# Two transformer layers on one core: other key blocks, more exponentials on VectorE, one GELU moved

## The chip, the cores and the metric

The kernel runs on one core of one Trainium2 chip. The metric is the device time of the core in microseconds (us), the median over several executions. Where two kernels are compared, both ran on the same chip in the same rounds. The chips used for the experiments were not all the same one, and the kernel before ran between 1080.2 and 1083.6 us (medians) on them, so between chips only ratios of the same rounds are compared. On one chip its executions went from 1080.5 us at a granted clock of 0.998 to 1086.9 at 0.992; single profiles therefore differ by a few us for no reason in the kernel.

## The reference, cut to what matters

Two identical layers on 2048 rows of 448 numbers. Each is an attention block (16 heads of 28) and a mixer block with two GELUs.

```python
def _A_ref(x, wqkv, wo):            # attention
    ...
    scores = jnp.einsum("bhqd,bhkd->bhqk", q, k) * (Dh ** -0.5)
    p = _softmax(scores, axis=-1)
    o = jnp.einsum("bhqk,bhkd->bhqd", p, v)
    return ... @ wo

def _B_ref(x, w1, w2, w3, w4):      # mixer
    h = _gelu(_layernorm(x) @ w1)
    # four quarters of h are shifted by -1, +1, -2, +2 rows: hs
    x1 = x + hs @ w2
    return x1 + _gelu(_layernorm(x1) @ w3) @ w4

x = x + _A_ref(_layernorm(x), wqkv, wo); x = x + _B_ref(_layernorm(x), w1, w2, w3, w4)   # twice
```

The softmax has 2 x 16 x 2048 x 2048 exponentials; they are the largest single piece of work. The second layer's attention needs keys from all rows of the first layer's output, so at the crossing the first layer's mixer has to deliver in time.

## The kernel before

Rows are cut into 16 tiles of 128, queries into units of four tiles, heads into four groups of four. TensorE makes scores (keys on the partitions, 512 queries wide) in groups of two or three 512-column banks; ScalarE turns each group into exponentials with one instruction; TensorE multiplies these with the values. A "segment" is one unit, one head group and one block of keys. The first units of a layer work on blocks of keys as these become known; what a block gives is stored and merged later with a correction factor:

```python
ORDER = {0: [(0, 0), (0, 1), (0, 2)], 1: [(0, 0), (1, 0), (0, 1), (0, 2), (1, 1), (1, 2)]}   # (unit, block)
PARTS = {0: [(0, 4), (4, 8), (8, NT)], 1: [(0, 8), (8, 12), (12, NT)]}                      # key tiles of a block
```

Some groups leave their third score to VectorE, which makes the exponential with integer and polynomial steps in seven instructions:

```python
def on_dve(n):
    if len(grans[n]) < 3:
        return False
    L, u, g, p, kts, first, last = segs[grans[n][2][0]]
    return 1 <= grans[n][2][1] <= len(kts) * UNITS[L][u][1] // 4 - 4 and (104 < n < 300 and n % 8 == 0)

def t_dexp(n):
    # ...
    yield op("dve", 0.06 + c_ps(512), lambda e: e.tensor_scalar(out=t32[:, :], in0=ps[:, bk, :], scalar1=0.0, scalar2=65536.0, op0=ALU.max, op1=ALU.mult), ...)
    # five instructions on 512 columns of fp16, then the seventh writes the bf16 result
```

The mixer's second GELU is run in batches of tiles, each between two loads of ScalarE's function table. In `MIXB` an entry is (tiles, ..., batch):

```python
MIXB = [
    [([0, 1, 2], 0, 0), ([3, 4, 5, 6], 3, 0), ([7, 8, 9, 10], 0, 1), ([11, 12], 4, 2), ([13, 14, 15], 0, 2)],
    [([0, 1, 2], 4, 0), ([3, 4, 5, 6], 0, 0), ([7, 8, 9, 10], 3, 1), ([11, 12], 0, 1), ([13], 2, None), ([14, 15], 3, None)],
]
```

The mixer's weights come by four loads on SyncE's queue during the first layer's attention. The queries' normalized rows `xn` are turned into `xT` by a transposing DMA on the same queue:

```python
for (dst, src_, nm, w) in ((w1, B_w1, "w1", 112), (w3, B_w3, "w3", 112), (w2, B_w2, "w2", 112), (w4, B_w4, "w4", 128)):
    yield op("sp", 0.1, lambda e, ...: e.dma_start(...), writes=[(nm,)], dma=True, dma_time=12.0)

def transposes(xs, xt, n, on_pe=False):
    # ...
    yield op("sp", 0.1, lambda e: e.dma_start_transpose(...), reads=[xs.key, ("xnpad",)], writes=[xt.key], dma=True, dma_time=2.4 + 0.65 * n)
```

The program is not written in the order in which it runs. Every task yields operations with an assumed duration; an order-maker places them on the engines by priority, and `MOVES` is a list of (time, random number) by which it shakes the priorities. Such lists are found by search: the one with the shortest estimate is kept. The order of each engine is then fixed: in the stall shown below, TensorE waits 9.23 us for one product, and the scores that stand behind it come only after it. Where the order-maker expects TensorE idle, it puts in dummy products with an all-ones tile. They are meant to keep its granted clock up.

```python
for k in range(ROUNDS):
    res = attempt(plan)
    plan = res[2].latest_starts(res[0])
for moves in MOVES[:-1]:
    res = attempt(plan, moves)
    plan = res[2].latest_starts(res[0])
est, P, SC = attempt(plan, MOVES[-1])
```

A DMA has a fixed duration there: 2.4 + 0.65 x 4 = 5.0 us for a transposing DMA of four tiles.

Of the kernel before, what the change touches and what calls it, by code (L numbers as in the profile page):

```python
# [8 lines left out]
ALU = mybir.AluOpType  # L9
# [487 lines left out]
def build_kernel(nc, A_x, A_wqkv, A_wo, B_x, B_w1, B_w2, B_w3, B_w4, out, n_layers=2):  # L497
# [13 lines left out]
    DEFER = 4  # L511
    EXPC = (0.30457565 * 128, 0.07826797 * 128)
# [6 lines left out]
            (0.00, 991188), (12.02, 9652), (24.07, 779245), (36.31, 574974), (48.34, 995852), (133.26, 234581), (170.16, 377973), (182.64, 78779),  # L519
            (194.78, 320468), (218.87, 670156), (268.25, 22056), (280.26, 710161), (292.73, 679129), (304.89, 711509), (328.97, 386094), (382.28, 899246),  # L520
            (406.49, 746217), (418.70, 101258), (430.88, 346142), (443.17, 682745), (455.33, 932794), (467.35, 356989), (479.51, 744780), (510.52, 543020),
            (522.57, 402041), (534.73, 618216), (546.82, 418518), (558.83, 824624), (570.92, 353463), (624.44, 145788), (636.47, 941956), (648.52, 565007),
            (684.71, 872168), (697.00, 394582), (709.22, 683072), (745.71, 487532), (757.79, 818477), (770.17, 569389), (806.55, 126763), (818.66, 378060),
            (870.93, 441302), (907.43, 514310), (919.45, 887013), (931.49, 271738), (968.02, 708052), (980.04, 674587), (992.15, 577414), (1004.20, 157345),
            (1016.21, 778514), (1028.52, 870529), (1040.65, 657776), (1052.77, 892667),
# [8 lines left out]
    ORDER = {0: [(0, 0), (0, 1), (0, 2)], 1: [(0, 0), (1, 0), (0, 1), (0, 2), (1, 1), (1, 2)]}  # L534
# [7 lines left out]
        [([0, 1, 2], 4, 0), ([3, 4, 5, 6], 0, 0), ([7, 8, 9, 10], 3, 1), ([11, 12], 0, 1), ([13], 2, None), ([14, 15], 3, None)],  # L542
# [8 lines left out]
    PARTS = {0: [(0, 4), (4, 8), (8, NT)], 1: [(0, 8), (8, 12), (12, NT)]}  # L551
# [19 lines left out]
    with st:  # L571
# [40 lines left out]
        kmaxc = sb("kmaxc", [128, 2, 4, NCH], FP32)  # L612
# [3 lines left out]
        dcol = sb("dcol", [128, 2, NPART, 4], FP32)  # L616
        dbc = sb("dbc", [128, 2, NPART, 4], FP32)
        fct = sb("fct", [128, 2, NPART, 4], FP32)
# [248 lines left out]

        def kslot(L, c):
            return c if L % 2 == 0 else (4, 5, 0, 1)[c]
# [7 lines left out]
        def norm_x(tiles, xs):  # L877
            for i, t in enumerate(tiles):
                yield op("dve", 0.12 + c_b2b(D), lambda e, t=t, i=i: e.tensor_scalar(out=blk(xs.v[:, i, :]), in0=b112(x_res[:, t, :]), scalar1=mv[:, t, 0:1], scalar2=rstd[:, t:t + 1],
                                                                          op0=ALU.subtract, op1=ALU.mult),  # L880
                         reads=[("x", t), ("mv", t), ("rstd", t)], writes=[(xs.key, i)])
# [51 lines left out]
        def k_proj(L, c, g, xt):  # L933
            c0 = kcol(L, 4 * c)
            b2 = yield from kq_proj(xt, g, wk_pad, "wk_pad", kT[:, g, c0:c0 + 512], [("kT", g, vslot(L, 4 * c + i)) for i in range(4)], MK, ("cols",), 512, 1.0)
            yield op("dve", c_ps(512), lambda e, b2=b2: e.reduce_max(out=kmaxc[:, L, g, c:c + 1], in_=ps[:, bi(b2), :], axis=AX.X),  # L936
# [4 lines left out]
        def q_proj(L, u, g, xt):  # L941
# [4 lines left out]
            if u >= PU[L]:  # L946
                yield ("wait", ("bc", L, NPART - 1, g))
                bias, bkey = bcol[:, L, NPART - 1, g:g + 1], ("bcol", L, NPART - 1, g)
# [30 lines left out]
        def t_ln1(L, c):  # L979
            tiles = list(range(4 * c, 4 * c + 4))  # L980
# [28 lines left out]
            sl = slice(4 * c, 4 * c + 4)  # L1009
            yield op("dve", 0.1, lambda e: e.tensor_scalar(out=vpe[:, sl], in0=mv[:, sl, 1], scalar1=EPS, scalar2=None, op0=ALU.add),  # L1010
                     reads=[("mv", t) for t in tiles], writes=[("vpe", t) for t in tiles])
            yield op("pool", 1.0, lambda e: e.tensor_tensor(out=rstd[:, sl], in0=vpe[:, sl], in1=neghalf[:, 0:4], op=ALU.pow),
# [728 lines left out]
```

## Time and profile before

| | kernel before |
|---|---|
| time, median of 3 | 1080.63 us (1080.58 to 1082.69) |
| span of the profiled execution, granted clock | 1077.6 us, 1.0 |
| ScalarE busy | 1028.3 us, 95% |
| first to last softmax exponential | 27.1 to 1041.6 us |
| from the last one to the end (below: the tail) | 36.1 us |

The span is read as three parts: up to the first exponential, the phase from the first to the last exponential, in which ScalarE is nearly always busy, and the tail. The lines for this stand in the prediction below. One thing the prediction did not look at, and that matters later, is SyncE's queue around 150 us, when the queries of unit 1 of the first layer are prepared. The lines of that queue's timeline in the kernel before have start, duration of the issue on the queue, what is issued, and how many:

```profile
134.81 1.73 SPq L798 DMA_DIRECT2D wo_pad<-in_A_wo_dram  x4
136.59 2.26 SPq L801 DMA_DIRECT2D w<-in_B_w_dram  x4
149.91 16.58 SPq L852 DMA_TRANSPOSE xT<-xn  x2
```

The four weight loads are issued from 136.59 us; the transposing DMA follows 13 us later (the line covers it and the next one, which starts at 165 us). The view of the tile `xT` for 120 to 240 us says how long its three transposing DMAs took from issue to landing:

```profile
DMA to landing us min/median/max: 3.2/3.6/8.2
```

Two took some 3.5 us, the one behind the loads 8.2. By the same view TensorE waited 2.2 us for it, and ScalarE's longest wait for a score (L1212), 1.9 us at 157 us, follows from that.

### The profile page before, as it was taken

The numbers are of one execution on the slowest core, as the hardware profiler recorded it, in microseconds if no ns is written. First come the engines' busy times: TensorE is split into PE (matmuls) and PEld (weight loads), VectorE is DVE, ScalarE is ACT, GpSimd is POOL, SyncE is SP. The second block draws the span as 40 slices with busy tenths as digits, with TensorE's granted clock in tenths as the row PEclk, the third lists the DMA queues.
The fourth block names the chain that finished last, engine by engine and source line by source line (L and its number), as shares of the span: only waits on it lengthen the run. The fifth ranks groups of instructions, "written<-read, shape, count | busy, mean of one in ns | idle before, by whom it ended". The sixth has DMA issues, their size and how long they took to land.

```text
span 1077.6 us, 22234 instructions
## 1 busy us (share of the span) xinstructions
PE 1041.8 (97%) x9674; PEld 407.6 (38%) x9674; DVE 649.5 (60%) x1539; ACT 1028.3 (95%) x939; POOL 54.3 (5%) x76
## 2 busy tenths in 40 slices
PE   8999999999999899999999999999999999999998
PEld 5233333333333333334334333333333333444545
DVE  7976148753885456933797338346958332755734
ACT  5999999999999999999999999999999999999973
POOL 2000000000000000000001000000000000010000
PEclk9999999999999999999999999999999999999999
DMA  4222080000000010000111112213110001100000
GB/s 114 60 89 69 10 194 20 16 1 21 20 2 20 2 40 21 1 21 20 21 40 31 26 40 60 69 35 113 46 28 4 21 14 29 21 21 2 2 15 26
DMA packets 74330, 37.85 MB, mean 35 GB/s; under 512 B 59064, under 2 KB 67640, under 8 KB 74232
## 3 DMA queue, kind: packets, MB, share of 16 engines
q1 hardware_dynamic: 74232, 36.43, 13.0%
q8 instruction: 75, 1.23, 0.5%
q14 instruction: 23, 0.19, 0.1%
HBM read 13.75 MB, written 8.13 MB: 20 GB/s over the span
## 4 chain that ended last, share of the span: by engine, by line
ACT 58%; PE 36%; DVE 4%; DMA 1%; issue 0%; SPq 0%; POOL 0%; DVEq 0%
ACT PT L1238 51%; PE ps L649 11%; PE ps L1212 10%; PE ps L1287 8%; ACT h2T L1615 4%; PE ps L652 4%; PE ps L1651 3%; ACT gt L1401 1%; ACT L1238 1%; ACT L1615 1%; DMA h2T<-in_A_wqkv_dram 1%; DVE st L811 0%; DVE qT L952 0%; DVE kmaxc L936 0%; DVE sq L924 0%
## 5 line engine op out<-in xcount | busy, mean ns | idle before, releaser
L1238 ACT ACTIVATE PT<-ps 128x1024 bf16<-128x1024 f32 (+1 forms) x823 | 930.1, 1243 | 14.1 <-PE ps L1212 10.3
L1212 PE MATMUL ps<-qT,kT 32*128 32x512 bf16 (+1 forms) x2304 | 320.1, 360 | 13.7 <-ACT PT L1238 9.3
L1287 PE MATMUL ps<-PT,vaug 128*32 128x512 bf16 (+1 forms) x2286 | 256.5, 362 | 3.4 <-ACT PT L1238 2.4
L1212 PEld LDWEIGHTS ps<-qT,kT 32*128 32x128 bf16 x2304 | 80.1, 91 | 261.2 <-ACT PT L1238 158.7
L1651 PE MATMUL ps<-ones_bf 128*128 128x256 bf16 x1136 | 171.3, 278 | 1.3 <-DVE hot L683 1.1
L1577 DVE CAST h2T<-ps 128x512 bf16<-128x512 f32 (+2 forms) x126 | 73.6, 584 | 97.8 <-PE ps L649 55.1
L1651 PEld LDWEIGHTS ps<-ones_bf 128*128 128x128 bf16 x1136 | 94.9, 99 | 77.8 <-issue 58.3
L1287 PEld LDWEIGHTS ps<-PT,vaug 128*32 128x32 bf16 x2286 | 66.0, 94 | 131.6 <-issue 75.5
L649 PE MATMUL ps<-xT,w 112*128 112x512 bf16 (+6 forms) x535 | 108.7, 323 | 0.9 <-DVE h2T L1577 0.2
L652 PE MATMUL ps<-xT,w 112*32 112x512 bf16 (+3 forms) x964 | 73.6, 339 | 0.0
L649 PEld LDWEIGHTS ps<-xT,w 112*128 112x128 bf16 (+1 forms) x535 | 43.1, 105 | 45.0 <-issue 20.9
L649 PE MATMUL ps<-w,h2T 128*128 128x448 bf16 x250 | 58.8, 354 | 1.3 <-ACT h2T L1615 1.3
L652 PE MATMUL ps<-w,h2T 128*32 128x448 bf16 x792 | 51.2, 353 | 6.0 <-ACT h2T L1615 5.5
L1315 DVE SCALAR_TENSOR_TENSOR uin<-uin,fct,ps 128x512 f32<-128x512 f32 x24 | 17.9, 745 | 57.3 <-PE ps L1287 55.1
L1594 DVE TENSOR_TENSOR uin<-x_res,ps 128x448 bf16<-128x448 bf16 x16 | 9.9, 620 | 60.0 <-PE ps L649 43.3
L1615 ACT ACTIVATE h2T<-h2T 128x7168 bf16<-128x7168 bf16 (+2 forms) x9 | 44.7, 5009 | 0.1
L811 DVE BATCH_NORM_STATS2 st<-x_res 128x6 f32<-128x448 bf16 x64 | 38.9, 614 | 1.6 <-DMA x_res<-in_A_x_dram 0.9
L1309 DVE STREAM_TRANSPOSE u_sb<-ps 128x512 f32<-128x512 f32 (+1 forms) x24 | 15.0, 626 | 37.2 <-PE ps L1287 37.1
L1601 DVE TENSOR_TENSOR x_res<-x_res,ps 128x448 bf16<-128x448 bf16 x16 | 9.8, 617 | 45.7 <-PE ps L652 26.8
L1536 POOL TENSOR_TENSOR mst<-mst,neghalf 128x1 f32<-128x1 f32 x32 | 22.9, 726 | 284.8 <-DVE mst L1534 284.8
L652 PEld LDWEIGHTS ps<-xT,w 112*32 112x32 bf16 (+1 forms) x964 | 30.1, 95 | 11.8 <-DVE h2T L1577 1.6
L1438 POOL TENSOR_TENSOR mst<-mst,neghalf 128x4 f32<-128x4 f32 (+2 forms) x10 | 9.1, 908 | 499.1 <-DVE mst L1437 351.7
(147 smaller groups left out, 969.7 us busy)
## 6 DMA issues: line engine op xcount, KB each, us to landing
uin<-uscr SPq DMA_DIRECT2D x24, 256.0 KB, 2.7
w<-in_B_w_dram SPq DMA_DIRECT2D x2, 1568.0 KB, 14.3
uscr<-u_sb SPq DMA_DIRECT2D x12, 256.0 KB, 2.0
uscr<-uin SPq DMA_DIRECT2D x12, 256.0 KB, 2.0
out_dram<-uin SPq DMA_DIRECT2D x16, 112.0 KB, 1.7
x_res<-in_A_x_dram SPq DMA_DIRECT2D x3, 448.0 KB, 8.7
h2T<-in_A_wqkv_dram SPq DMA_DIRECT2D x2, 392.0 KB, 5.8
w<-in_B_w_dram SPq DMA_DIRECT2D x2, 392.0 KB, 9.7
```

What stands on the lines that cost most here:

```text
L649: return e.matmul(out=dst(0, m), lhsT=lhs(0, m), rhs=rhs, start=start, stop=stop)
L652: return [e.matmul(out=dst(a, min(m, a + 32)), lhsT=lhs(a, min(m, a + 32)), rhs=rhs, start=start, stop=stop, tile_position=(0, a)) for a i ...
L811: yield op("dve", 0.55, lambda e: e.bn_stats(out=st6[:, t, :], in_=x_res[:, t, :]), reads=[("x", t)], writes=[("st6", t)])
L1212: yield op("pe", 0.005 if ph == h else 0.012 + W / 2400.0, lambda e, bk=bk, r0=32 * j, g=g, kc=kc, q0=q0, W=W, c0=W * h: e.matmul(out=ps[: ...
L1238: yield op("act", e_dur(n), lambda e, b0=b0, p0=p0, cnt=cnt: e.activation(out=PT[:, p0:p0 + cnt, :], in_=ps[:, b0:b0 + cnt, :], func=ACT.E ...
L1287: yield op("pe", nt * 0.054 if item in late else 0.004 + nt * 0.0133, lambda e, j=j, rhs=rhs, vs=vs, i=i: e.matmul(out=ps[32 * j:32 * j + ...
L1309: yield op("dve", c_ps(W), lambda e: e.transpose(out=u_sb[:, 0:W], in_=ps[:, UBK, 0:W]), reads=[("ps", UBK)], writes=[("u",)], last=[("ps" ...
L1315: yield op("dve", 0.06 + c_ps(W), lambda e: e.scalar_tensor_tensor(out=uin[:, :], in0=uin[:, :], scalar=fct[:, L, p, g:g + 1], in1=ps[:, U ...
L1536: yield op("pool", 0.57, lambda e, t=t: e.tensor_tensor(out=mst[:, t, R3:R3 + 1], in0=mst[:, t, V3E:V3E + 1], in1=neghalf[:, 0:1], op=ALU. ...
L1577: yield op("dve", c_ps(NW), lambda e, fch=fch, b=b: e.tensor_copy(out=h2T[:, fch, hoff:hoff + NW], in_=ps[:, bi(b), 0:NW]), reads=[("ps", ...
L1615: yield op("act", c_act(14 * NW), lambda e, c0=c0, NW=NW: e.activation(out=h2T[:, :, c0:c0 + NW], in_=h2T[:, :, c0:c0 + NW], func=ACT.Gelu ...
L1651: SC.fill = (0.13, lambda e, b: e.matmul(out=ps[:, bi(b), 0:256], lhsT=ones_bf[:, :], rhs=ones_bf[:, :].unsqueeze(1).to_broadcast([128, 2, ...
```

## The change

Its intent, by parts:

1. 39 third scores instead of 18 go to VectorE, to take work off ScalarE.
2. The second layer's key blocks become 7, 3 and 6 tiles (unit 1: 10 and 6), because the first layer's GELU batches finish tiles 0-6, then 7-10, then 11-15: a block should not wait for one tile of a later batch.
3. K is projected in pieces of 4, 3, 1, 2, 2 and 4 tiles to match. Pieces of one or two tiles are transposed on TensorE.
4. The last layer's GELU of tiles 11-12 is run after the last exponential instead of before it.
5. Two assumed durations are corrected, and the list of `MOVES` is a new one, so the whole program is ordered anew.

```diff
+    OFFL = ((48, 104, 6), (104, 150, 8), (150, 204, 6), (204, 300, 8), (500, 600, 8), (640, 731, 6))
...
-            (0.00, 991188), (12.02, 9652), (24.07, 779245), ...
+            (0.00, 453789), (24.05, 533123), (36.08, 574974), ...
...
-    ORDER = {0: [(0, 0), (0, 1), (0, 2)], 1: [(0, 0), (1, 0), (0, 1), (0, 2), (1, 1), (1, 2)]}
+    ORDER = {0: [(0, 0, 4), (0, 4, 8), (0, 8, 16)],
+             1: [(0, 0, 7), (1, 0, 10), (0, 7, 10), (0, 10, 16), (1, 10, 16)]}
+    KCH = [[(4 * c, 4) for c in range(NCH)], [(0, 4), (4, 3), (7, 1), (8, 2), (10, 2), (12, 4)]]
...
-        [([0, 1, 2], 4, 0), ([3, 4, 5, 6], 0, 0), ([7, 8, 9, 10], 3, 1), ([11, 12], 0, 1), ([13], 2, None), ([14, 15], 3, None)],
+        [([0, 1, 2], 4, 0), ([3, 4, 5, 6], 0, 0), ([7, 8, 9, 10], 3, 1), ([11, 12], 0, 2), ([13], 2, None), ([14, 15], 3, None)],
...
-    PARTS = {0: [(0, 4), (4, 8), (8, NT)], 1: [(0, 8), (8, 12), (12, NT)]}
+    ENDS = [sorted(set(b for (_, _, b) in ORDER[L])) for L in range(2)]
...
-                yield op("dve", 0.12 + c_b2b(D), lambda e, t=t, i=i: e.tensor_scalar(out=blk(xs.v[:, i, :]), ...
+                yield op("dve", 0.21 + c_b2b(D), lambda e, t=t, i=i: e.tensor_scalar(out=blk(xs.v[:, i, :]), ...
...
-            yield from transposes(xs, xt, 4)
+            yield from transposes(xs, xt, n, n <= 2)
...
-            return 1 <= grans[n][2][1] <= len(kts) * UNITS[L][u][1] // 4 - 4 and (104 < n < 300 and n % 8 == 0)
+            return 1 <= grans[n][2][1] <= len(kts) * UNITS[L][u][1] // 4 - 4 and any(a <= n < b and n % m == 0 for (a, b, m) in OFFL)
...
-            yield op("act", c_act(nw), lambda e: e.activation(out=tt, in_=w, func=ACT.Tanh, scale=2 * math.sqrt(2 / math.pi)),
+            yield op("act", 0.09 + nw * 0.0011, lambda e: e.activation(out=tt, in_=w, func=ACT.Tanh, scale=2 * math.sqrt(2 / math.pi)),
...
+            after = L == n_layers - 1 and batch[0][0] >= NT - 6
+            if after:
+                yield ("wait", ("e", len(grans) - 1))
```

The rest of the diff carries the block ends and pieces through the program (sizes of small tiles, loops, waits) and is left out here.

## The prediction

> **What bounds the kernel now.** I read, in this order: busy shares and slices of the page, the chain that ended last, ScalarE's instructions by form, its waits, the stretches of time, and the timeline of the last 75 us.
>
> From the page, shares and slices:
>
> ```profile
> PE 1041.8 (97%) x9674; PEld 407.6 (38%) x9674; DVE 649.5 (60%) x1539; ACT 1028.3 (95%) x939; POOL 54.3 (5%) x76
> ...
> ACT  5999999999999999999999999999999999999973
> PEclk9999999999999999999999999999999999999999
> ```
>
> Two engines look full. TensorE's 97% is not its need: the group of dummy multiplications with the all-ones tile (below) is 1136 instructions and 171 us that are issued only to keep it busy. ScalarE has no such padding: it is short of work only in the first slice and the last two. The chain of the page agrees (shares of the span):
>
> ```profile
> ACT 58%; PE 36%; DVE 4%; DMA 1%; issue 0%; SPq 0%; POOL 0%; DVEq 0%
> ...
> L1651 PE MATMUL ps<-ones_bf 128*128 128x256 bf16 x1136 | 171.3, 278 | 1.3 <-DVE hot L683 1.1
> ```
>
> What ScalarE does, by form (busy us, mean ns of one, idle before):
>
> ```profile
> L1238 ACT ACTIVATE PT<-ps 128x1536 bf16<-128x1536 f32 x392 | 575.9, 1469 | 10.0 <-PE ps L1212 6.7 <-PE ps L1287 2.6
> L1238 ACT ACTIVATE PT<-ps 128x1024 bf16<-128x1024 f32 x423 | 438.7, 1046 | 4.1 <-PE ps L1212 3.6 <-PE ps L1287 0.3
> ...
> L1615 ACT ACTIVATE h2T<-h2T 128x3584 bf16<-128x3584 bf16 x2 | 6.4, 3184 | 0.0
> ```
>
> 823 softmax exponentials, of three, two or one 512-column scores. One more score costs 1469 - 1046 = 423 ns. Instructions overlap: 50 of them, alternately three and two, take 56.53 us in the chain from 941.98, 1.131 each; so the step is about 0.073 + 0.423 per score. These exponentials run from 27.1 to 1041.6 us. What they wait for there is small:
>
> ```profile
> ACT PT L1238 <- PE ps L1212: 10.3, 17, 1.9
> ACT PT L1238 <- PE ps L1287: 2.9, 3, 2.2
> ```
>
> 13.2 us in 20 waits. The same view of 400 to 690 us alone gives 6.1 + 2.2 = 8.3 of them: the crossing from layer 1 to layer 2. VectorE by stretch (columns: length, then busy of PE, PEld, DVE, ACT, POOL):
>
> ```profile
> 80.00:120.00 40.00, 39.14 (x310) 14.93 (x311) 19.89 (x52) 40.00 (x38) 0.00 (x0) 1.00 0.17 47
> 120.00:160.00 40.00, 37.56 (x303) 14.66 (x304) 15.12 (x35) 38.06 (x35) 0.27 (x1) 1.00 0.58 138
> ...
> 800.00:840.00 40.00, 37.87 (x319) 14.81 (x316) 31.97 (x73) 40.00 (x39) 3.05 (x4) 1.00 0.12 27
> 840.00:920.00 80.00, 78.13 (x849) 28.69 (x846) 24.39 (x42) 79.01 (x62) 0.00 (x0) 1.00 0.05 15
> ...
> 1041.60:1077.60 36.00, 32.15 (x347) 22.11 (x345) 18.87 (x47) 12.94 (x38) 4.45 (x7) 1.00 0.07 23
> ```
>
> VectorE is half idle where ScalarE has nothing to spare; in the last 36 us the roles turn: ScalarE mostly waits, TensorE works. The timeline of ScalarE there:
>
> ```profile
> 1019.16 1.28 ACT L1615 ACT_TABLE_LOAD   x1
> 1020.45 9.26 ACT L1615 ACTIVATE h2T<-h2T 128x7168 bf16<-128x7168 bf16 x2
> 1029.73 1.28 ACT L1238 ACT_TABLE_LOAD   x1
> 1031.03 10.57 ACT L1238 ACTIVATE PT<-ps 128x1024 bf16<-128x1024 f32 x10
> 1041.61 1.28 ACT L1456 ACT_TABLE_LOAD   x1
> 1048.42 0.89 ACT L1456 ACTIVATE hT<-ps 112x128 bf16<-112x128 f32 x4 [5.53 <-PE ps L649]
> ```
>
> The 9.26 us hold the GELU of tiles 7-10 and, 3.1 us of it, of tiles 11-12. After the last table load ScalarE idles 5.53 us.
>
> **What the Trainium skill says.** "ScalarE: Activation LUTs", What ACT_TABLE_LOAD costs: an ACTIVATE takes 186 ns + 0.833 ns per column, neighbours overlap by about 93 ns, and a table load takes 1283 ns. Agrees: 186 + 1280 = 1466 against 1469 here; loads 1.28 us. It adds a drain of 1.38 us to each switch; here the GELU starts 1.29 us after its load starts, so I count 1.3. "VectorE: DVE Perf Modes", The perf-mode tier table: a PSUM operand keeps a 32-bit VectorE operation at 1x, so 512 columns cannot go below 533 ns; here such a read takes 688. "Perfetto Trace Analysis", Identifying the Most-Contended Engine: matmul busy share does not measure TensorE's need, occupancy of ScalarE does; the 171 us of dummies are the trace's evidence.
>
> **The change part by part.** I counted exponentials by going through the two segment lists by hand-written loops over the program's grouping rule (groups alternate 3 and 2 scores and are broken where the key bound changes); nothing was scheduled.
>
> *1. More exponentials on VectorE.* Old rule: every 8th group between 104 and 300 that has three scores and whose third score is not near a segment's edge: 18, which is the x18 of the trace. New list: 4 in groups 48-104, then 12 in 104-204 where there were 8, 10 in 204-300 as before, 3 in 500-600, 10 in 640-731: 39. So 21 more, 21 x 0.423 = 8.9 us off ScalarE, all on its full stretch. On VectorE one costs 688 + 420 + 291 + 424 + 293 + 425 + 685 ns = 3.2 us (its seven groups), 21 x 3.2 = 68 us more. The new ones lie at about 90-235, 690-760 and 800-905 us, where VectorE is busy 20/40, 15/40, 70/110 and then 32/40 and 24/80. TensorE: a late score's product is one lone 512-column multiplication instead of a quarter of a packed four, about 0.216 - 0.06 = 0.16 us more, 3 us in all, out of the dummies.
>
> *2. Key blocks 7, 3, 6 in layer 2.* Groups 823 to 821 (eight one-score groups become three): 2 x 0.073 = 0.15 us. Partial segments of layer 2 fall from 24 to 20, so the merges with the stored partial output (745 ns, x24) become x20 and the stores and loads 24 to 20: -4 x (0.75 + 0.69) = -6 us of VectorE, none of it on the path. The gain meant is the dependence: layer 1's GELU batches finish tiles 0-6, then 7-10, then 11-15. The old first block of 8 tiles needs tile 7, that is the second batch; the new one of 7 needs only the first, and 10 needs the second. Of the 8.3 us of waits in the crossing I expect a third to a half back: 3 us. Many of them are 0.2 to 0.6 us, which is order, not missing data.
>
> *3. K projected in 4,3,1,2,2,4.* Six chunks for four, x 4 head groups: 8 more sets of scale, square, reduce. From 748 against 476 ns for 512 and 256 columns the fixed part of a scale is some 0.2; 0.5 us a set by the three, 4 us more on VectorE. Chunks of one or two tiles are transposed on TensorE instead of by DMA: 5 copies at 0.42 us. All beside ScalarE: 0.
>
> *4. GELU of tiles 11-12 to the end.* -3.1 us from before the last exponential. It runs behind the table load already there, in the 5.53 us hole: 0 added for ScalarE. No table load saved or added. Then TensorE: before, 36 of the 84 fourth-layer multiplications of tiles 7-12 were still to do after 1041.6 (78 in the tail less 42 of tiles 13-15; four packed ones counted as one). Now at least the 28 of tiles 11-12 are, and those of 7-10 can be done earlier. 8 x 0.19 = 1.5 us less at best; but a wait for the late GELU can eat it. I put -0.5.
>
> *5. New order seeds and two better durations in the order search* (tanh, normalization): the program is ordered anew throughout. No number: it is the width of my range.
>
> Sum: -8.9 - 0.15 - 3.1 - 3 - 0.5 = -15.6 us; less 1 us given back by new waits for VectorE: -14.6. **1080.6 - 14.6 = 1066 us** (-1.35%).
>
> **Rivals.** (a) VectorE becomes a bound. In 800-840 it is busy 80%, and a 3.2 us exponential every 6 groups (6.8 us) asks for 47% more; the score's bank must be emptied by VectorE before the group after next may be written, so a late VectorE stops TensorE and then ScalarE. For it: the 1.9 us wait at 157 us lies where an offloaded score is being done beside four normalizations. Against: no wait over 0.3 us between 690 and 1041, and 840-920 is nearly empty, so other work can move. If true, 0.2 us of wait per new one, 4 us: 1070. (b) The crossing closes almost completely, as intended, and new ordering removes other waits: -8 instead of -3, 1060. (c) The tail grows: it is TensorE's (32.2 of 36 us), and moved work is added to the end one for one: +4, 1070. Against: 1.5 to 5 us of ScalarE's wait there is free. (d) The gain is all hidden because TensorE is really the bound: then 1080. Against: the dummies.
>
> **Range and chances.** Parts 1 and 4, 12 us, are near certain; waits can be anywhere from 6 to 17 us in place of 13, the tail +-3. So 1058 to 1073 holds it 8 times in 10. Faster by over 2% means below 1059.0: it needs (b) with no new wait and a shorter tail; 0.14. Slower by over 2%: 0.01. Within: 0.85.
>
> **What would show it.** VectorE's first read of a score counts x39 and each of its seven groups keeps its duration; the three-score form falls from x392 to 370, the two-score form rises to 448; the sum of all exponentials falls by 9 us. Merges x20. ScalarE's waits for TensorE from the first to the last exponential come to 8 to 12 us, less in the crossing. Last exponential about 1027; the tail from there 35 to 36 us, with the 3.2 us GELU directly after the last table load. Wrong if waits on TensorE that follow VectorE's reads of scores pile up at 800-840, if the tail exceeds 38 us, or if the first exponential moves from 27.1 us by more than 1.

## The result, and the profile after

| | before | changed |
|---|---|---|
| time, median of 4, same rounds | 1080.62 us (1080.58 to 1082.69) | 1083.83 us (1083.51 to 1085.93) |
| ratio, 95% interval | 1 | 1.0029 (1.0012 to 1.0046) |
| span of the profiled execution, granted clock | 1077.6 us, 1.0 | 1082.0 us, 0.992 |

The changed kernel is 0.3% slower: the same within 2%, as the prediction held most likely, but at 1083.8 us outside its range of 1058 to 1073.

The page of the changed kernel: shares and slices, then two groups.

```profile
PE 1030.9 (95%) x9448; PEld 401.7 (37%) x9462; DVE 711.7 (66%) x1712; ACT 1020.9 (94%) x934; POOL 58.2 (5%) x78
...
ACT  5999969999999999999999999999999999999973
...
PEclk9999989999999999999999999999999999999999
...
L1148 DVE TENSOR_SCALAR t<-ps 128x512 int32<-128x512 f32 x39 | 26.8, 686 | 29.2 <-PE ps L1234 29.0
```

ScalarE has 7.4 us less work, as intended (1028.3 to 1020.9), VectorE 62.2 us more, and the first of the seven VectorE instructions counts x39. But the sixth slice, 135 to 162 us, has fallen to 6 for ScalarE, and the granted clock to 8. In the table of waits of ScalarE:

```profile
ACT PT L1260 <- PE ps L1234: 19.1, 20, 9.9
ACT PT L1260 <- PE ps L1309: 0.8, 1, 0.8
```

One wait of 9.9 us. ScalarE's instructions by form (busy, mean of one, idle before):

```profile
L1260 ACT ACTIVATE PT<-ps 128x1536 bf16<-128x1536 f32 x370 | 540.6, 1461 | 8.8 <-PE ps L1234 7.1
L1260 ACT ACTIVATE PT<-ps 128x1024 bf16<-128x1024 f32 x448 | 456.9, 1037 | 13.6 <-PE ps L1234 12.0 <-PE ps L1309 0.8
```

370 and 448 are the counts that the prediction worked out; the durations did not change. So the work went away as counted, and time came back elsewhere. By stretches (length, then busy of PE, PEld, DVE, ACT, POOL, then the granted clock, DMA share, GB/s):

```profile
120.00:160.00 40.00, 30.40 (x221) 11.47 (x219) 17.14 (x37) 29.89 (x28) 0.00 (x0) 0.87 0.57 137
...
150.00:156.50 6.50, 0.01 (x1) 0.01 (x1) 0.50 (x2) 0.00 (x0) 0.00 (x0) 0.50 1.08 245
156.50:160.00 3.50, 3.50 (x17) 0.82 (x17) 1.35 (x2) 1.02 (x1) 0.00 (x0) 0.50 0.00 0
...
1042.30:1082.00 39.70, 34.93 (x380) 23.60 (x380) 20.34 (x52) 15.91 (x38) 4.78 (x7) 1.00 0.06 22
```

From 150.0 to 156.5 us the compute engines stand nearly still while the DMA engines are full (245 GB/s). From 156.5 to 160 us TensorE works at a granted clock of 0.50. And the tail is 39.7 us, not 36.1. TensorE's timeline at the stall:

```profile
156.49 1.89 PE L652 MATMUL ps<-xT,wq_pad 112*128 112x512 bf16 x4 [9.23 <-DMA xT<-xn]
158.31 0.60 PE L1234 MATMUL ps<-qT,kT 32*128 32x512 bf16 x2
```

TensorE waits 9.23 us for the transposed queries, then makes their first product, and only then the scores that ScalarE has been waiting for. SyncE's queue in the changed kernel, which answers to the lines shown of before:

```profile
136.41 2.12 SPq L804 DMA_DIRECT2D w<-in_B_w_dram  x4
141.37 13.00 SPq L855 DMA_TRANSPOSE xT<-xn  x1
```

The same four loads go out at the same time, but in the new order the transposing DMA follows after 5 us instead of 13. Its issue alone takes 13.00 us on the queue, and it lands 15.1 us after its start (against 8.2):

```profile
DMA to landing us min/median/max: 3.2/3.6/15.1
```

The Trainium skill says in "Perfetto Trace Analysis", Summary: the profiler window per engine type, that the window of a DMA issued from SyncE covers the wait for the descriptor generator and the generation and push of its descriptors, not the movement of the data. This agrees with the trace: landing comes 2.1 us after the window's end, here as in a run below where nothing is in the way (1.60 us of issue, 3.7 to landing). So the delay lies within the window of the issue and not after it; in "DMA: Bandwidth & Descriptors", Queues, rings and completion order, the skill says that each DMA engine consumes the descriptors of a queue in ring order, which fits a transposing DMA that stands behind four loads in the same queue. What the issue waited for inside its window is not visible here; the end of section A has a pattern that says when the wait ends.

The whole difference, from the two traces. "Exponentials" is the sum of 0.073 + 0.423 us per score over all groups; "other work" is the GELU, tanh, table loads and a few small instructions of ScalarE in the phase; "idle" is the gaps between ScalarE's instructions in the phase; the rest is mostly neighbours that overlap less after a gap.

| us | before | changed | difference |
|---|---|---|---|
| up to the first exponential | 27.1 | 28.2 | +1.1 |
| exponentials | 918.8 | 909.7 | -9.1 |
| other work in the phase | 78.8 | 75.3 | -3.5 |
| idle, 120 to 180 us | 1.9 | 10.8 | +8.9 |
| idle, 400 to 690 us (crossing) | 8.9 | 7.8 | -1.1 |
| idle, elsewhere in the phase | 4.0 | 5.0 | +1.0 |
| rest of the phase | 2.0 | 5.5 | +3.5 |
| tail | 36.1 | 39.7 | +3.6 |
| span | 1077.6 | 1082.0 | +4.4 |

### The profile page after: what moved, and what is told of

It reads as the page before. It is cut to its first block, busy times and chain, and to the rows that moved or that the text cites. A ratio compares the mean times of both kernels' runs of the same rounds, so it can differ in the third digit from the quotient of the medians. Undisturbed runs are those within 1.5% of the kernel's fastest.

```text
span 1082.0 us, 21948 instructions
## 1 busy us (share of the span) xinstructions
PE 1030.9 (95%) x9448; PEld 401.7 (37%) x9462; DVE 711.7 (66%) x1712; ACT 1020.9 (94%) x934; POOL 58.2 (5%) x78
## 4 chain that ended last, share of the span: by engine, by line
ACT 54%; PE 36%; DVE 6%; DMA 3%; issue 1%; SPq 0%; DVEq 0%
ACT PT L1260 48%; PE ps L652 10%; PE ps L1234 9%; PE ps L1309 8%; PE ps L1677 5%; ACT h2T L1641 4%; PE ps L655 3%; DMA xT<-xn 1%; DVE hT L1428 1%; ACT L1641 1%; DMA h2T<-in_A_wqkv_dram 1%; ACT gt L1424 1%; DVE hT L1397 1%; ACT L1260 0%; DVE h2T L1600 0%
## 5 line engine op out<-in xcount | busy, mean ns | idle before, releaser
L1309 PE MATMUL ps<-PT,vaug 128*32 128x512 bf16 (+1 forms) x2264 | 260.9, 362 | 3.6 <-ACT PT L1260 2.2
L1677 PE MATMUL ps<-ones_bf 128*128 128x256 bf16 x990 | 152.7, 279 | 2.5 <-DVE hot L686 1.1
L652 PE MATMUL ps<-xT,w 112*128 112x512 bf16 (+6 forms) x536 | 113.1, 326 | 1.1 <-DVE h2T L1600 0.3
L1677 PEld LDWEIGHTS ps<-ones_bf 128*128 128x128 bf16 x990 | 82.2, 99 | 75.7 <-issue 55.8
L652 PE MATMUL ps<-w,h2T 128*128 128x448 bf16 x314 | 74.4, 354 | 2.7 <-ACT h2T L1641 2.7
L1148 DVE TENSOR_SCALAR t<-ps 128x512 int32<-128x512 f32 x39 | 26.8, 686 | 29.2 <-PE ps L1234 29.0
L655 PE MATMUL ps<-w,h2T 128*32 128x448 bf16 x536 | 38.3, 369 | 2.4 <-ACT h2T L1641 2.4
L652 PE MATMUL ps<-xT,wq_pad 112*128 112x512 bf16 (+1 forms) x109 | 29.9, 374 | 10.1 <-DMA xT<-xn 9.2
L652 PEld LDWEIGHTS ps<-w,h2T 128*128 128x128 bf16 x314 | 26.9, 98 | 32.0 <-issue 12.9
```

Source lines behind the costliest of these rows:

```text
L652: return e.matmul(out=dst(0, m), lhsT=lhs(0, m), rhs=rhs, start=start, stop=stop)
L655: return [e.matmul(out=dst(a, min(m, a + 32)), lhsT=lhs(a, min(m, a + 32)), rhs=rhs, start=start, stop=stop, tile_position=(0, a)) for a i ...
L1309: yield op("pe", nt * 0.054 if item in late else 0.004 + nt * 0.0133, lambda e, j=j, rhs=rhs, vs=vs, i=i: e.matmul(out=ps[32 * j:32 * j + ...
L1677: SC.fill = (0.13, lambda e, b: e.matmul(out=ps[:, bi(b), 0:256], lhsT=ones_bf[:, :], rhs=ones_bf[:, :].unsqueeze(1).to_broadcast([128, 2, ...
```

## The experiments

**Theories.** A: the stall at 150 us is a matter of the place of the weight loads in the queue, which came with the new order, not of any of the four parts; without it the changed kernel is faster than before (0.6% was expected). Rivals: it comes with the parts (VectorE's new exponentials at 90 to 235 us delay the normalizations), and moving the loads changes nothing; or the wait goes but is made up elsewhere, because TensorE is the bound. B: taking 21 exponentials off ScalarE is worth 8.9 us. Rivals: VectorE has become a bound and takes it back; or TensorE's fixed order supplies scores no faster. C: the longer tail is the GELU's move. Rival: it is a matter of the order.

### A: the place of the weight loads

*a_wlate.* The changed kernel with its order kept; the four loads are only put behind the next transposing DMA of SyncE's queue, after the order is made.

```diff
         est, P, SC = attempt(plan, MOVES[-1])
+        late = [o for o in P.ops["sp"] if o.fn.__defaults__ and any(o.fn.__defaults__[0] is w for w in (w1, w3, w2, w4))]
+        nxt = P.ops["sp"][P.ops["sp"].index(late[-1]) + 1]
+        for lst in (P.ops["sp"], P.all):
+            for o in late:
+                lst.remove(o)
+            k = lst.index(nxt) + 1
+            lst[k:k] = late
```

> The changed kernel with one edit after its order has been made: on SyncE's queue the four feed-forward weight loads (w1, w3, w2, w4) stand behind the transposing DMA of unit 1's queries instead of in front of it; every other engine's order is the same. Theory A (the 9.9 us ScalarE wait at 149 us is that transposing DMA stuck behind 4 MB of weight loads): it lands in 3 to 6 us instead of 15.1, the wait goes from 9.9 to under 1 us, and the time falls by 9 to 10.5 us to 1073.5-1075, so 0.6% faster than before. Theory B (the wait is VectorE, which had two exponentials and the output merge there): the wait stays over 5 us and the time falls by under 3. Theory C (the wait is made up elsewhere because TensorE is the real bound): wait gone but time falls by under 4.

Measured: 1072.99 us, ratio to before 0.9899 (0.9877 to 0.9921). SyncE's queue, and then the table of ScalarE's waits, of this run:

```profile
141.54 1.60 SPq L855 DMA_TRANSPOSE xT<-xn  x1
143.18 2.25 SPq L804 DMA_DIRECT2D w<-in_B_w_dram  x4
165.83 1.59 SPq L855 DMA_TRANSPOSE xT<-xn  x1
```

```profile
ACT PT L1260 <- PE ps L1234: 8.5, 18, 1.6
```

The transposing DMA starts at the same 141.5 us; its issue takes 1.60 instead of 13.00 us, its landing at most 3.7 instead of 15.1, and the 9.9 us wait is gone. The span is 1070.9, 11.1 shorter than the changed kernel's: 11.0 of it is ScalarE's idle time in the phase (23.6 to 12.6). Both rivals are out: VectorE's work is the same, and the time fell by more than the 4 us that the second one allowed. The same kernel was run again as a companion of later runs (a_wlate2): 

> a_wlate once more, as the control of a_pad21 on the same chip: ratio to before 0.988-0.992.

Measured: 1073.47 us, 0.991 (0.9876 to 0.9943). It repeats.

*a_w4late.* The same edit with `(w4,)` in place of `(w1, w3, w2, w4)`: only the last load, one of the two large ones (1568 KB), is moved. It is a smaller dose.

> Dose: the changed kernel with only the last of the four loads (w4, 1.6 MB of 4) behind the transposing DMA. Theory A: the landing time falls in proportion to what is left in front of it, 15.1 us to about 9-11, the wait to 4-6 us, the time by 4 to 6 us. If the stall is a fixed cost of a transposing DMA that meets any load, the wait stays 9 to 10 us.

Measured: 1080.12 us, 0.9968 (0.9943 to 0.9993). The issue of the transposing DMA took 8.51 us, its landing 11.4, ScalarE's wait 6.2. A part of the dose gives a part of the wait: with landings of 15.1, 11.4 and at most 3.7 us, ScalarE's wait is 9.9, 6.2 and none. The difference between landing and wait is 5.2 us twice: that much slack the order has there.

*b_collide.* The reverse: in the kernel before, the loads are held back until just ahead of the transposing DMA.

```diff
+        norm = [o for o in P.all if o in nxt.every and o.eng == "dve"]
+        norm = sorted(norm, key=lambda o: o.pos)[0]
+        late[0].deps[norm.ekey] = norm
+        for o in late:
+            P.all.remove(o)
+        k = P.all.index(norm) + 1
+        P.all[k:k] = late
```

> The reverse in the kernel before: the four loads are held back until the first normalization of unit 1's queries, about 1 to 3 us ahead of the transposing DMA, as in the changed kernel; no other order is touched. Theory A: the DMA takes 13 to 16 us to land, ScalarE's wait there grows from 1.9 to 8-11 us and the time by 6 to 9 us to 1087-1090, although nothing of the change is in it. Theories B and C: under 2 us.

Measured: 1092.32 us, 1.0071 (1.004 to 1.0103). SyncE's queue in this run:

```profile
148.48 1.92 SPq L801 DMA_DIRECT2D w<-in_B_w_dram  x4
150.62 14.49 SPq L852 DMA_TRANSPOSE xT<-xn  x1
```

The issue took 14.49 us and the landing 16.4, and the longest wait of ScalarE was 10.5. So the old kernel, without any of the change, gets the same stall and loses some 8 us by it.

*b_wlate.* The first edit on the kernel before: does its own 1.9 us wait go too?

> The same edit in the kernel before, whose transposing DMA came 13 us after the loads, took 8.2 us to land and made a 1.9 us wait. Theory A: -1.5 to -2 us, to 1078.7-1079. Theories B and C: no change. Together with the previous run it says what the whole change is worth without the collision: theory A expects the changed kernel to be 4 to 5 us (0.4%) faster then.

Measured: 1084.23 us, 1.0017 (0.999 to 1.0045), so no gain, and my expectation of a small one missed. The 1.9 us wait is gone (ScalarE runs without a gap from 149.17 to 173.49 us), so it did come from the transposing DMA. The queue shows why nothing is gained (the profile is of the longest execution, 1090.17 us): the first transposing DMA is issued in 1.60 us, but the loads then go out at 154.87 and meet the next transposing DMA at 166.51, which takes 6.16 us to issue and 8.1 to land; waits of 3.3 us and less follow. In this order the moved loads are closer to the next customer (11.6 us) than in a_wlate (22.7 us).

What follows for A: the theory holds, in both kernels. From the first of the four loads to the transposing DMA it is 2.1 us in b_collide, 5.0 in the changed kernel, 11.6 in b_wlate, 13.3 in the kernel before and 22.7 in a_wlate's second one; the landings are 16.4, 15.1, 8.1, 8.2 and at most 3.7 us. The traces show one thing more. The issue of the delayed transposing DMA ends 0.2 to 0.35 us before the last load in front of it lands, in each of the runs: 154.59 against 154.89 us in the kernel before, 154.37 against 154.71 in the changed one, 151.10 against 151.41 in a_w4late, 165.11 against 165.34 in b_collide, 172.67 against 172.86 in b_wlate. The last of the four loads lands 16.9 to 18.3 us after the first is issued. So in this program the delay was what was left of these 17 to 18 us when the transposing DMA's turn came. Why the issue waits for the loads is not shown. The search that found the new order could not see it, because the order-maker gives the transposing DMA its fixed 5.0 us.

### B: what the exponentials taken off ScalarE are worth

*b_less21.* The kernel before, in which 21 three-score groups near those of the new list simply leave out their third score. Nothing is added to VectorE. The result is wrong (relative error 0.088), the order is kept.

```diff
+        LESS = (54, 66, 84, 96, 104, 162, 174, 198, 512, 552, 560, 648, 654, 660, 672, 678, 684, 696, 702, 708, 720)
+        # cut: these, or the neighbour where one has two scores
+        for n in cut:
+            b0, p0, cnt = main[n].fn.__defaults__
+            main[n].fn.__defaults__ = (b0, p0, 2)
```

> The kernel before, order untouched, with ScalarE told to do only two of the three scores in 21 groups about where the change takes scores away (groups 54-104, 162-198, 512-560, 648-720). VectorE gets nothing instead, so the result is wrong on purpose. It is the best that part 1 of the prediction could give in this order: 21 x 0.423 = 8.9 us. If ScalarE is the bound in all these places (prediction's view): -8 to -9 us, ScalarE's idle time stays near 15 us. If TensorE's fixed order takes over (rival d): idle time between first and last exponential grows by 3 us or more and the time falls by only 3 to 6 us.

Measured: 1081.23 us, 0.9985 (0.9949 to 1.0021). ScalarE's forms in this run:

```profile
L1238 ACT ACTIVATE PT<-ps 128x1536 bf16<-128x1536 f32 x371 | 544.9, 1469 | 13.7 <-PE ps L1212 10.4 <-PE ps L1287 2.6
L1238 ACT ACTIVATE PT<-ps 128x1024 bf16<-128x1024 f32 x444 | 456.4, 1044 | 5.6 <-PE ps L1212 4.7 <-PE ps L1287 0.3
```

21 x 0.423 = 8.9 us were taken away, and the span fell by 1.7 (1077.6 to 1075.9, both at a granted clock of 1.0). The interval of the ratio goes from 5.5 us faster to 2.3 slower: it leaves open whether anything was gained, but not a gain of 8.9. 5.5 us came back as idle time of ScalarE (14.8 to 20.3) and 1.7 as lost overlap. Its waits for scores (the two groups of before had 10.0 and 4.1 us of idle) rose to 13.7 and 5.6. VectorE had nothing to do with it, so rival (a) of the prediction falls as the main cause. ScalarE gets to the next score earlier, and TensorE has not made it yet: rival (d), in the form "TensorE's fixed order", holds for most of the gain. My expectation with that rival was a larger rest than the 1.7 found.

*a_pad21.* The opposite dose: a_wlate, in which 21 groups are followed by a dummy ScalarE instruction of 396 columns. It takes 0.42 us in a row of exponentials (527 ns alone).

```diff
+        for n in PAD:      # the same 21 numbers
+            pad = _Op("act", lambda e, n=n: e.activation(out=PT[:, gblk(n) + 2, 0:396]..., in_=ones_bf[:, 0:99]..., func=ACT.Identity), False)
+            pad.pos = main[n].pos
+            for lst in (P.ops["act"], P.all):
+                lst.insert(lst.index(main[n]) + 1, pad)
```

> a_wlate, order of all real work untouched, with a dummy ScalarE instruction of 396 columns (about 0.42 us a step) behind 21 of the 23 groups that are newly offloaded: it gives ScalarE back what part 1 of the change took from it, while VectorE keeps its extra work. If those 8.9 us are worth their face value: +8 to +9 us over a_wlate2 of the same rounds. If most of them had gone into waits for TensorE: +2 to +5 us, and ScalarE's idle time falls from 12.6 us by 4 us or more.

Measured: 1082.59 us, 0.9994 (0.9957 to 1.0031), 9.1 us more than a_wlate2 of the same rounds. So adding work to ScalarE costs its full size, and taking it away gave a fifth by the spans. An order that was searched for a certain load of ScalarE is tight on both engines.

*With the order made anew.* In the changed kernel the order was made for the smaller load, so a trial by order is needed. *t_nooffl* is the changed kernel with the old 18 exponentials on VectorE and its own list of `MOVES`, found by the same kind of search of some thousand orders. Its loads lie 13 us ahead of the transposing DMA, and they were left there.

```diff
-    OFFL = ((48, 104, 6), (104, 150, 8), (150, 204, 6), (204, 300, 8), (500, 600, 8), (640, 731, 6))
+    OFFL = ((105, 300, 8),)
-            (0.00, 453789), (24.05, 533123), ...
+            (0.00, 66172), (12.03, 567712), ...
```

> The changed kernel with the old list of VectorE exponentials (18 or 19 of them), ordered anew by the same search; loads where the order puts them, 15 us ahead of the transposing DMA. If an offloaded score is worth its 0.423 us on ScalarE with no new waits: sum of exponentials 8.9 us higher than in the changed kernel, waits in all no lower, time 6 to 11 us above a_wlate (ratio to before 0.995-1.002). If VectorE's load makes waits that eat the gain: within 3 us of a_wlate.

Measured: 1072.82 us, 0.9913 (0.9881 to 0.9946): level with a_wlate, with 8.9 us more of ScalarE's work. One order is one draw. *t_nooffl2* is a second search from other seeds; *t_nooffl_n1* and *t_nooffl_n2* continue the two searches by more than 3,000 orders each; *t_full_m1* is the full change, with 39, by an independent search of 5,200 orders and the loads placed as in a_wlate. Against t_nooffl (for t_full_m1: against a_wlate) their edit is the list of `MOVES` alone.

> The same configuration as t_nooffl (changed kernel with the old list of VectorE exponentials) in an order from an independent search of the same length; its weight loads stand about 15 us ahead of the transposing DMA. If t_nooffl's equality with a_wlate is a property of the configuration: ratio to before 0.989-0.994 and ScalarE idle time of 4 to 8 us again. If it was the luck of one order: ratio 0.996 or more, idle time over 10 us.

> The whole change in an order from an independent search (5,200 orders), loads behind the transposing DMA. With a_wlate and a_wlate_tail it is the second independent order of the full change. If the exponentials moved to VectorE are worth something once the order is made for it: ratio to before 0.985 or less, 4 us or more under t_nooffl_n1 and t_nooffl_n2. If not: 0.988-0.994.

> The changed kernel with the old list of VectorE exponentials, t_nooffl's order searched on for 3,200 orders (mainly a shorter tail). Expect ScalarE idle time of 5 to 8 us, tail 37 to 39 us, ratio to before 0.988-0.992: as good as the full change with 21 fewer VectorE exponentials. Over 0.994: t_nooffl was luck.

> The same for t_nooffl2's order, 3,700 further orders. Same expectation: 0.988-0.993. If both stay level with t_full_m1 within 3 us, the 8.9 us of ScalarE work taken away buys nothing in this program; if t_full_m1 is 4 us or more faster than both, it buys about half its face value or more.

| VectorE makes | kernel | ratio (95%) | median us | exponentials us | idle after 130 us | of it 400 to 690 | tail us |
|---|---|---|---|---|---|---|---|
| 39 | a_wlate | 0.9899 (0.9877 to 0.9921) | 1072.99 | 909.7 | 11.5 | 7.9 | 39.7 |
| 39 | a_wlate2, the same again | 0.991 (0.9876 to 0.9943) | 1073.47 | 909.7 | 13.1 | 8.9 | 39.7 |
| 39 | a_wlate_tail (below) | 0.9911 (0.9883 to 0.994) | 1071.74 | 909.7 | 11.0 | 6.4 | 37.0 |
| 39 | t_full_m1 | 0.9912 (0.9849 to 0.9974) | 1074.93 | 909.7 | 9.2 | 4.7 | 38.5 |
| 18 | t_nooffl | 0.9913 (0.9881 to 0.9946) | 1072.82 | 918.6 | 4.4 | 1.8 | 39.8 |
| 18 | t_nooffl2 | 0.9919 (0.9879 to 0.9959) | 1074.20 | 918.6 | 5.7 | 1.6 | 38.6 |
| 18 | t_nooffl_n1 | 0.9888 (0.9836 to 0.994) | 1071.92 | 918.6 | 6.1 | 3.0 | 38.3 |
| 18 | t_nooffl_n2 | 0.9899 (0.9847 to 0.995) | 1073.22 | 918.6 | 5.5 | 1.6 | 38.0 |

The two halves are level: 0.9899 to 0.9912 against 0.9888 to 0.9919. An effect of 8.9 us would be 0.8%. Where the work went is visible in ScalarE's idle time from 130 us to the last exponential (before that, the orders trade an earlier first exponential for more waiting behind it): 9.2 to 13.1 us with 39, 4.4 to 6.1 with 18, in the mean 11.2 against 5.4. So with 18, ScalarE's larger work comes with 5.8 us less idle time, most of it in the crossing (7.0 against 2.0). The rest is in the start, the tail and the overlaps, and differs from order to order. These are fewer independent draws than rows: a_wlate2 and a_wlate_tail have a_wlate's order (but for the tail), and the last two rows continue the two above them, so it is two orders against two. In the rounds that they share, t_full_m1's median is 3.0 and 1.7 us above those of t_nooffl_n1 and t_nooffl_n2. Within what these draws can tell, the 21 exponentials are worth about nothing.

### C: the GELU and the key blocks

*t_nogelu.* The changed kernel (loads placed as in a_wlate) with the GELU of tiles 11-12 back in the batch of tiles 7-10, searched anew over about 5,000 orders.

```diff
-    ... ([7, 8, 9, 10], 3, 1), ([11, 12], 0, 2), ...
+    ... ([7, 8, 9, 10], 3, 1), ([11, 12], 0, 1), ...
-            after = L == n_layers - 1 and batch[0][0] >= NT - 6
+            after = False
```

> The changed kernel with the GELU of tiles 11-12 put back into the batch of tiles 7-10 (so before the last exponentials), ordered anew by the same random search of some 5,000 orders, weight loads behind the transposing DMA as in a_wlate (1% faster than before). Theory T (moving the GELU gives its 3.1 us back: the last 36-40 us are TensorE's, and w3 and w4 products of tiles 7-12 that lay beside exponentials now lie there): last exponential ends 2 to 4 us later than in a_wlate (about 1033-1035), the tail from there is 3 to 4.5 us shorter (35-36.5 instead of 39.7), total within 2 us of a_wlate, ratio to before 0.988-0.992. The prediction's view (the moved GELU is free in the tail): ratio 0.993 or more, tail equal.

Measured: 1076.45 us, 0.9971 (0.993 to 1.0012), so the expected ratio of 0.988 to 0.992 was missed. The tail is 35.0 us, about as expected, 4.7 shorter than a_wlate's; the phase is 11.1 us longer (1014.0 against 1002.9). Of these, only some 3.2 are the GELU itself; 6.7 are more idle time (19.3 against 12.6), and 7.8 of the 19.3 lie before 130 us, where nothing of this edit acts. First exponential and idle time before 130 us together are 33.6 us here and 29.4 in a_wlate, 4.2 more, and the spans differ by 3.9 (1074.8 and 1070.9). Apart from that poor start the two are level, which argues that the move is worth about nothing; it does not show it, as each is one draw of an order.

What the tail gained in the changed kernel is seen in ScalarE's timeline there:

```profile
1017.95 6.18 ACT L1641 ACTIVATE h2T<-h2T 128x7168 bf16<-128x7168 bf16 x1
...
1042.30 1.28 ACT L1641 ACT_TABLE_LOAD   x1
1045.44 3.19 ACT L1641 ACTIVATE h2T<-h2T 128x3584 bf16<-128x3584 bf16 x1 [1.86 <-DVE h2T L1600]
1050.80 1.28 ACT L1479 ACTIVATE hT<-ps 112x128 bf16<-112x128 f32 x4 [2.17 <-PE ps L652]
```

The GELU before the last exponentials is 3.1 us shorter, as planned. The moved one waits 1.86 us for VectorE's copies of its input, because 7 of its third-layer products are now made in the tail too: the fourth-layer products left to TensorE there rise from 78 to 87 and the third-layer products from 112 to 119 (four packed ones counted as one). In columns that is 72,384 to 78,272. In these traces products of 448 columns follow each other every 189 ns, 0.42 ns a column, so 5,888 columns are an estimated 2.5 us of the 3.6; TensorE's busy time in the tail rose by 2.8 (32.15 to 34.93).

*a_wlate_tail.* a_wlate with only the part of `MOVES` after 950 us searched again.

> a_wlate with its last order seeds (after 950 us) searched anew, 1,700 orders; the order up to about 920 us is the same. If the tail is bound by TensorE's work there, it shortens only by what can be moved ahead of the last exponential: 1 to 3.5 us, total 1 to 3 us under a_wlate (ratio to before 0.987-0.989), and TensorE's work in the tail falls with it. If it is a chain of latencies, the tail stays 39 to 40 us.

Measured: 1071.74 us, 0.9911 (0.9883 to 0.994). The tail is 37.0 instead of 39.7 us and TensorE has 73,344 columns there; the span of its profile is 1068.9, the shortest of all. So both readings of C are half right: 2.7 us were the order's, and the 2.0 left against t_nogelu's 35.0 us may be the move's. All orders together say the same: with the GELU before the last exponential the tails are 35.0, 36.1 and, in t_noblocks below, 37.0 us; with it after, 37.0 to 39.8. The ratio does not differ from a_wlate's.

*t_noblocks.* Besides the GELU, the key blocks are put back to 8, 4 and 4 tiles and K to pieces of four; order searched anew, loads placed as in a_wlate.

```diff
-             1: [(0, 0, 7), (1, 0, 10), (0, 7, 10), (0, 10, 16), (1, 10, 16)]}
-    KCH = [[(4 * c, 4) for c in range(NCH)], [(0, 4), (4, 3), (7, 1), (8, 2), (10, 2), (12, 4)]]
+             1: [(0, 0, 8), (1, 0, 8), (0, 8, 12), (0, 12, 16), (1, 8, 12), (1, 12, 16)]}
+    KCH = [[(4 * c, 4) for c in range(NCH)], [(4 * c, 4) for c in range(NCH)]]
```

> More VectorE exponentials alone: key blocks 8, 4, 4 and K in chunks of four as before, GELU as before, ordered anew by the same search, loads behind the transposing DMA. If the key blocks are worth what they are meant for: ScalarE waits between 400 and 690 us of 8 us or more, and a time 4 to 10 us above t_nogelu. If they are worth nothing (as the unchanged waits of the crossing in the changed kernel's trace suggest): within 2 us of t_nogelu. Sum of exponentials as in the changed kernel (39 on VectorE).

Measured: 1075.14 us, 0.9938 (0.9906 to 0.9971): in the same batch of runs its median is 1.3 us below that of t_nogelu, which has the new blocks, so by this expectation the blocks are worth nothing. TensorE's timeline of this run at the crossing, then ScalarE's:

```profile
506.25 3.01 PE L651 MATMUL ps<-w,h2T 128*128 128x448 bf16 x15
509.10 1.03 PE L651 MATMUL ps<-xT,wk_pad 112*128 112x512 bf16 x4
...
510.44 0.82 PE L1308 MATMUL ps<-PT,vaug 128*32 128x512 bf16 x10
```

```profile
510.87 3.72 ACT L1259 ACTIVATE PT<-ps 128x1536 bf16<-128x1536 f32 x3 [6.05 <-PE ps L1308]
```

Fifteen fourth-layer products of a mixer batch and the K projection that needs its result stand ahead of the value products, and ScalarE waits 6.05 us in one piece: this is the dependence the new blocks are meant to ease. With the new blocks no wait is of this size; but the kernel before has the old blocks too, and its longest wait there is 2.2 us, so the order has its share. The crossing's idle time is 8.9 us in the kernel before and 7.9 in t_noblocks. With the new blocks it is 7.8 in the changed kernel, 7.9 in a_wlate (8.9 when repeated), 6.4 in a_wlate_tail, 5.2 in t_nogelu and 4.7 in t_full_m1, all with 39 exponentials, and 1.6 to 3.0 in the four orders with 18. So the new blocks go with less idle time there in most orders, but not in all, and the time of the whole kernel does not show it.

All runs gave a correct result, but for b_less21.

## Why the prediction was wrong

Predicted -14.6 us, measured +3.2 by the medians and +4.4 by the profiled spans. By its own steps:

**Step 5, the new order, "No number: it is the width of my range".** This is the step that failed first. The new order put the transposing DMA 5 us behind the weight loads, and ScalarE's idle time there rose by 8.9 us, with a granted clock of 0.50 after it. The experiment that moves the loads gives 11.1 us of span back and makes the kernel 1% faster than before. At a_wlate's ratio of 0.9899 the change would have come to 1069.7 us, within the range; but that would have been luck for step 1, as orders without its exponentials come to the same. A range of 15 us around the sum of the other parts treated an order as noise of a few waits of a microsecond; one collision was as large as the largest of the four parts. The hint was in the profile: the kernel before had its longest wait for a score, 1.9 us, at exactly this place, with a landing of 8.2 us against 3.6. The prediction saw that wait and put it down to VectorE (rival a).

**Step 1, more exponentials on VectorE, -8.9 us.** The count (39, 370 and 448) and the duration (0.423 us per score) were right, and ScalarE's sum fell by 9.1 with the fewer groups. The value was wrong: 1.7 us in the old order without any cost on VectorE, about nothing between re-searched orders. The step that failed is the dismissal of rival (d) with the words "Against: the dummies". TensorE's 171 us of dummies are an average over the whole span; by stretches the trace of the kernel before has 30.8 us of them from 100 to 200 us, but 7.1 from 500 to 600 and none in the tail. Re-searched orders have 5.8 us more idle time of ScalarE with the smaller work, most of it in the crossing, and the 7.1 us from 500 to 600 us lie there. Which products in the order hold the scores back there is not settled.

**Step 4, the GELU at the end, -3.1 and -0.5.** The 3.1 us are there (other work in the phase fell by 3.5). The tail was mis-sized: +3.6 instead of -0.5. Rival (c), +4, was right in size, in part by luck: TensorE's added work, an estimated 2.5 us, is what it named, but another order of the tail (a_wlate_tail) is 2.7 us shorter with the GELU still at the end. The free 5.53 us of ScalarE were not free for the products that follow the GELU.

**Step 2, the key blocks, -3 us.** -1.1 us in the changed kernel, with merges x20 and stores as counted. In other orders with the same blocks it is 0 to -4.2 with 39 exponentials and -5.9 to -7.3 with 18, and -1.0 in t_noblocks with the old blocks. So the 3 us lie within what an order decides, and what the blocks alone give stays open. **Step 3**, K in more pieces, was put at 0 and nothing contradicts it; it was not tried alone.

**The sign tests.** The prediction named what would show it wrong: a tail over 38 us (39.7), and a first exponential that moves by more than 1 us (27.1 to 28.2, just over). Both came, but the second says nothing about the change: the granted clock of the first 27 us was 1.00 in the profile of the kernel before and 0.94 in that of the changed one, and runs that share the old kernel's order up to there have the first exponential at 27.8 us with 0.94 (b_collide) and at 30.6 with 0.81 (b_wlate). Waits piling up at 800 to 840 us behind VectorE, the sign of rival (a), did not come. One reading was off without harm: the prediction lets an overlap of neighbouring exponentials of about 93 ns pass as in agreement, where its own lines give 127 ns ((1469 + 1046) / 2 - 1131); its step of 0.073 + 0.423 us was taken from the trace.

Still, the change is worth something: with the loads placed safely, full or with only 18 exponentials on VectorE, it is 0.8 to 1.1% faster than the kernel before. The best ratio, 0.9888 of t_nooffl_n1 (1071.92 us), and a_wlate's 0.9899 beat both kernels and are not told apart by their intervals. That half of these versions lack the extra exponentials says that the gain comes from the rest (blocks, GELU, a fresh order, load placement); how it divides among these is open. t_noblocks, with neither the blocks nor the GELU's move, already has 0.9938, and no run searched the unchanged kernel anew, so a fresh order and two better durations may account for much of it.

## What to carry to other kernels

A part's saving on the busiest engine is an upper limit, and in a program whose order was searched until two engines are tight it can be nearly zero; test it by taking the work away (even with a wrong result) before building the replacement. When a change makes a program be ordered anew, compare the order of the DMA queue with its landings as well as the engines: a model with fixed DMA times can place a small urgent transfer right behind large ones without noticing, as it did here. How long the large ones take to land, here 17 to 18 us, says how far off is safe. Work moved to the end of a program joins whichever engine runs there; size the tail by that engine.

## What the Trainium skill lacked or had wrong

- "DMA: Bandwidth & Descriptors", Rules for kernel authors: it says that a transpose next to ordinary DMAs needs nothing. It says so of corrupted data, and for the result it held in every run made to be correct; of the time it says nothing: 5 us behind four weight loads, a transposing DMA of four tiles took 13.00 us to issue and 15.1 to land, against 1.60 and at most 3.7 ahead of them. I found no page with a distance or a cost for this.
- "Perfetto Trace Analysis", Identifying the Most-Contended Engine: it says to optimize the engine of highest occupancy first. ScalarE was at 95%, and taking 8.9 us off it shortened the span by 1.7. The rule lacks the case of two engines that a fixed order ties together.
- "ScalarE: Activation LUTs", Rules for kernel authors: for `exp` it says that ScalarE is the only option. Here seven VectorE instructions (3.2 us, by the durations in the prediction) make the exponential of 128 x 512 scores, with a correct result, 39 times.
- "ScalarE: Activation LUTs", What ACT_TABLE_LOAD costs: the drain of 1.38 us that it adds to each switch is not seen: in the kernel before, the last exponential ends at 1041.60 us and the table load starts at 1041.61; after the load that starts at 1029.73 the next exponential starts at 1031.03, 1.30 later.
